# Twenty-four further loads of V behind the last DMA transpose, ahead of eleven output stores on one queue

## The chip, the cores and the metric

The kernel runs on one core of a Trainium2 chip. The core has a matrix engine (TensorE, PE in the profile), a vector engine (VectorE, DVE), a scalar engine (ScalarE, ACT), GpSimd (POOL) and SyncE (SP), which issues almost all DMAs here. The engines run side by side and each works through its own instructions in order; between engines only semaphores order the work. Sixteen DMA engines move data between HBM and SBUF. The metric is the device time of one execution in microseconds (us), lower is better.

## The reference

One block of a transformer with conditioned layer norms, 2048 positions of 512 features in bfloat16. What is computed:

```python
mod = (_silu(c) @ w_mod).reshape(c.shape[0], 6, 1, -1)      # sa, ca, ga, sb, cb, gb
h = _layernorm(x) * (1 + ca) + sa
x = x + ga * _A_ref(h, A_wqkv, A_wo)      # attention
h = _layernorm(x) * (1 + cb) + sb
x = x + gb * _B_ref(h, B_w1, B_w3, B_w2)  # silu(h @ w1) * (h @ w3) @ w2, inner width 1792
```

The attention has 32 heads of 16 features, and each position sees eight positions only, itself and those 2, 4, ... 14 before it:

```python
idx = pos[:, None] - off[None, :]         # off = arange(8) * 2
vg = v[:, :, idx_c, :].reshape(B, H, S, W, Dh)
o = jnp.einsum('bhsw,bhswd->bhsd', attn, vg)
```

## The kernel before, in words

The positions are cut into 16 tiles T of 128. Layer norm, projections to Q, K and V, attention, the second layer norm and the two-layer network are each written as functions over tiles or groups of tiles, which record operations (`Program.op`, `Program.dma`) with what they read and write. The order of all operations and the buffer that each value gets are then not decided when the kernel is built: they stand in two long lists, ORDER and SLOTS (L952 and L998). `place` follows them, `synchronize` derives the waits on semaphores from them, and `emit` (L208) writes, for every engine, its operations in that order, each with its waits ahead of it. So each engine, SP included, has one fixed sequence.

V goes through HBM: after its projection each tile is stored to `v_scratch_dram` (L695), and the attention loads it back with the eight needed rows beside each other (L790). One such load is 128 runs of 2 KB (256 KB), and four make a tile's buffer `sb_vsh` of 128 x 8 x 512; there are two of these buffers, `vshb`, and a third in the space of the finished weights (`sb_vshx`). In each load a row of V is read up to eight times, since neighbouring positions need the same rows.

At the end stand the network's two layers. L853 multiplies the activations with w1 or w3 (four 128x256 matmuls make one group and fill half a PSUM bank), L859 on ACT and L862 on DVE turn two groups into one `sb_hh`, and L891 or L879 multiply these with w2. L901 on DVE adds the residual and writes an output buffer `sb_o`, and SP stores it:

```python
p.op("dve", lambda e: e.tensor_tensor(vo.at[:, 0:n], bank(vz)[:, 0:n], x_sb[:, T, c0:c0 + n], ALU.add),
     c_dve(n), ("zo", T), r=[vz, vx[T]], w=[vo])
finals.append(p.dma(out2d[T * P:(T + 1) * P, c0:c0 + n], lambda: vo.at[:, 0:n], ("zo", T), (128, 2 * n), r=[vo], cost=400, store=True))
```

There are four output buffers, called here the first to the fourth, and eight PSUM banks. A value that gets a buffer or a bank waits for all users of the value that had it before (`o.prev` in `place`).

The end of the sequences matters for the change. SP has, as its last entries: four DMA transposes of `sb_xn` into `sb_h` (for the second layer norm of tiles 12 to 15, the last of them being the program's last transpose); then the stores of the tiles 9 (from the fourth output buffer), 11 (second), 10 (third), 12 (third), 13 (second), 1 (first) and 8 (fourth); then four stores of half tiles, two each of tiles 14 and 15. DVE has the L901 of tiles 10, 9 and 11, then of tile 8, which writes the fourth output buffer again, then those of tiles 13 and 12, then four for the halves; the L862 lie between them. The L901 of tile 8 reads PSUM bank 1. The next user of that bank on PE is an L853 group for tiles 14 and 15: the eighth group of four behind the w2 matmuls (L891) that the trace starts at 213.20.

Of the kernel before, what the change touches and what calls it, by code (L numbers as in the profile page):

```python
# [10 lines left out]
P = 128  # L11
S = 2048
D = 512
H = 32
DH = 16
W = 8
DIL = 2
# [4 lines left out]
PAD = 16  # L22
# [51 lines left out]
class Program:  # L74
# [133 lines left out]
    def emit(self):  # L208
        nc = self.nc
        with nc.Block() as block:  # L210
            starter = {"sp": block.sync, "pe": block.tensor, "dve": block.vector, "act": block.scalar,
                       "pool": block.gpsimd}
            for eng in ENGINES:
                todo = self.order[eng]
                if not todo:
                    continue

                def section(e, todo=todo, eng=eng):
                    for o in todo:
                        for d in o.waits:  # L220
                            e.wait_ge(d.inc[0], d.inc[2])
                        ins = o.fn(e)
                        if o.inc is not None:
                            ins.then_inc(o.inc[0], o.inc[1])
                    if eng == "sp":
                        for d in self.final:
                            e.wait_ge(d.inc[0], d.inc[2])

                starter[eng](section)

# [5 lines left out]
def bass_adaLN_cond__sliding_local_dilated__glu_gated_swiglu__prompt_kernel(  # L236
    nc, A_x, A_wqkv, A_wo, B_x, B_w1, B_w3, B_w2, c, w_mod, out
):
    ctx = ExitStack()
    with ctx:  # L240
        p = Program(nc, ctx)
        _build(p, *[_full_ap(t) for t in (A_x, A_wqkv, A_wo, B_w1, B_w3, B_w2, c, w_mod, out)])
        p.place(ORDER, SLOTS)
        p.synchronize()
        p.emit()
# [27 lines left out]
def _build(p, A_x, A_wqkv, A_wo, B_w1, B_w3, B_w2, c, w_mod, out):  # L273
    nc, ctx = p.nc, p.ctx
# [5 lines left out]
    def sb(shape, dtype, name):  # L280
        return ctx.enter_context(nc.sbuf_tensor("sb_" + name, shape, dtype))
# [12 lines left out]
    vshb = [sb([P, 8, D], bf, f"vsh{i}") for i in range(2)]  # L294
# [44 lines left out]
    v_dram = nc.dram_tensor("v_scratch_dram", (PAD + S, D), bf)  # L339
# [97 lines left out]
    for g in range(NG):  # L437
# [8 lines left out]
         r=[vthc, vcT], w=[vc4])  # L446
# [3 lines left out]
         r=[vc4, vident] + wm_hold, w=[vpc])  # L450
# [494 lines left out]
    for o, n in zip(p.late, GATES):  # L945
        if n >= 0:
            o.deps[p.gates[n]] = True
    p.final = finals


GATES = [-1, -1, -1, -1, -1, -1, -1, -1, -1, 1, -1, -1, -1, -1, -1, 1, -1, -1, 2, -1]
# [94 lines left out]
```

## Time and profile before

| what | us |
|---|---|
| median of 2 runs | 243.95 (242.89 to 245.02) |
| the profiled execution, device time | 243.86 |
| its span, first to last instruction | 242.0 |
| PE busy | 232.3 |
| DVE busy | 180.0 |
| ACT busy | 135.6 |
| last transpose issued | 199.04 |
| first output store behind it issued | 210.31 |

The span is what the profile's times count from; the device time has 1.86 us more around it. "Busy" counts an engine's compute instructions; waits and the issuing of DMAs are not counted, so SP, which only waits and issues, appears with its issues alone (as SPq). A line such as L853 is the line of the kernel that made the instruction. In a timeline row the first number is the start, the second the time that the row covers, and "x" the count of instructions merged in it; an idle time before the row and what ended it stand in brackets. In the sums by window the busy times of the engines follow each other, and the last three columns are the granted TensorE clock, the busy share of the DMA engines and the GB/s that they moved.

### The profile page before, as it was taken

What the parts mean: (1) busy time and instruction counts of PE and PEld (TensorE: products, weight loads), DVE (VectorE), ACT (ScalarE), POOL (GpSimd) and SP (SyncE); (2) the same over time, 40 slices, a digit from 0 to 9 for tenths busy, and PEclk for the clock granted to TensorE, in tenths of its full rate; (3) what the DMA queues carried; (4) which work ended last, traced back from release to release, by engine and by line L of the source; (5) the groups of instructions that cost most, each with busy time, mean ns of one, the idle gap of its engine ahead of it and who ended that gap; (6) DMA issues with size and microseconds to landing.
All of it is one profiled execution on the core that took longest, in us unless ns stands there. A gap on an engine that the chain in (4) does not pass through costs nothing.

```text
span 242.0 us, 4516 instructions
## 1 busy us (share of the span) xinstructions
PE 232.3 (96%) x1778; PEld 135.8 (56%) x1803; DVE 180.0 (74%) x278; ACT 135.6 (56%) x269; POOL 23.2 (10%) x66
## 2 busy tenths in 40 slices
PE   7999999979899999999999999999999999999995
PEld 2667454434368777674444454444444555768864
DVE  4689999968899999999999999928443611433532
ACT  2178498757979743794774479262476334314200
POOL 4144110002003000040000012000010100000000
PEclk9999999999999999999999999999999999999999
DMA  6998999899999879698292189674031010010004
GB/s 219 385 355 286 172 257 264 132 253 261 305 323 285 228 199 237 148 270 176 71 242 80 33 172 240 141 174 131 3 103 27 0 24 22 23 45 0 3 0 130
DMA packets 45756, 38.84 MB, mean 160 GB/s; under 512 B 21656, under 2 KB 36520, under 8 KB 45736
## 3 DMA queue, kind: packets, MB, share of 16 engines
q1 hardware_dynamic: 45728, 38.56, 61.6%
q8 instruction: 14, 0.23, 0.4%
q14 instruction: 6, 0.05, 0.1%
q10 hardware_dynamic: 8, 0.00, 0.0%
HBM read 29.62 MB, written 4.21 MB: 140 GB/s over the span
## 4 chain that ended last, share of the span: by engine, by line
PE 73%; DVE 13%; DMA 6%; SPq 3%; ACT 1%; issue 1%; POOL 0%; DVEq 0%; ACTq 0%
PE pall L853 39%; PE pall L891 17%; DVE sb_pq L712 5%; PE pall L837 4%; DMA sb_vsh<-v_scratch_dram 3%; SPq L124 3%; PE pall L825 2%; PE pall L497 2%; PE pall L879 2%; DVE sb_vsh L797 2%; DVE sb_st L534 2%; DMA sb_wo<-in_A_wo_dram 2%; DMA v_scratch_dram<-sb_v 2%; PE pall L722 2%; PE pall L661 1%
## 5 line engine op out<-in xcount | busy, mean ns | idle before, releaser
L853 PE MATMUL pall<-sb_h,sb_w 128*128 128x256 bf16 (+1 forms) x665 | 102.7, 307 | 0.9 <-ACT sb_sg L859 0.4
L853 PEld LDWEIGHTS pall<-sb_h,sb_w 128*128 128x128 bf16 x672 | 64.6, 98 | 36.0 <-issue 1.3
L859 ACT ACTIVATE sb_sg<-pall 128x256 bf16<-128x256 f32 (+1 forms) x84 | 35.1, 455 | 49.1 <-PE pall L853 44.4
L862 DVE TENSOR_TENSOR sb_hh<-sb_sg,pall 128x256 bf16<-128x256 bf16 (+1 forms) x84 | 39.6, 506 | 29.0 <-PE pall L853 27.1
L891 PE MATMUL pall<-sb_w,sb_hh 128*128 128x512 bf16 x187 | 43.3, 379 | 0.5
L712 DVE TENSOR_TENSOR sb_pq<-sb_q,sb_kT 128x4096 bf16<-128x4096 bf16 x16 | 36.4, 2285 | 0.0
L661 PE MATMUL pall<-sb_h,sb_wqkv 128*128 128x512 bf16 (+1 forms) x156 | 31.6, 335 | 1.6 <-ACT sb_h L591 0.7
L797 DVE TENSOR_TENSOR sb_vsh<-sb_vsh,sb_al 128x4096 bf16<-128x4096 bf16 x13 | 29.7, 2288 | 3.2 <-DMA sb_vsh<-v_scratch_dram 1.9
L891 PEld LDWEIGHTS pall<-sb_w,sb_hh 128*128 128x128 bf16 x196 | 19.0, 98 | 20.7 <-issue 0.4
L591 ACT ACTIVATE sb_h<-sb_h,sb_modc 128x512 bf16<-128x512 bf16 (+1 forms) x24 | 16.4, 737 | 15.7 <-DMA sb_h<-sb_xn 15.6
L661 PEld LDWEIGHTS pall<-sb_h,sb_wqkv 128*128 128x128 bf16 x160 | 14.7, 98 | 13.6 <-ACT sb_h L591 1.3
L901 DVE TENSOR_TENSOR sb_o<-pall,sb_x 128x512 bf16<-128x512 f32 (+1 forms) x18 | 11.1, 628 | 14.4 <-PE pall L891 11.7
L681 PE MATMUL pall<-sb_wqkv,sb_h 128*128 128x512 bf16 x63 | 16.5, 379 | 0.1
L837 PE MATMUL pall<-sb_wo,sb_ot 128*128 128x512 bf16 x61 | 15.6, 379 | 1.0 <-DMA sb_ot<-sb_ac 0.8
L556 POOL TENSOR_SCALAR sb_nm<-sb_sx 128x2 f32<-128x2 f32 x8 | 2.7, 332 | 129.0 <-DVE sb_x L841 129.0
L614 ACT ACTIVATE sb_h<-pall,sb_modc 128x256 bf16<-128x256 bf16 (+1 forms) x18 | 10.3, 629 | 7.8 <-PE pall L606 7.8
L831 ACT ACTIVATE sb_ac<-pall 128x512 bf16<-128x512 f32 x16 | 9.4, 601 | 7.6 <-PE pall L825 7.5
L571 ACT ACTIVATE sb_xn<-sb_x,sb_nb,sb_rs 128x512 bf16<-128x512 bf16 x16 | 12.6, 810 | 1.6 <-POOL sb_nb L569 1.4
L841 DVE SCALAR_TENSOR_TENSOR sb_x<-pall,sb_x 128x512 bf16<-128x512 f32 x16 | 10.7, 686 | 3.6 <-PE pall L837 3.6
L534 DVE BATCH_NORM_STATS2 sb_st<-sb_x 128x6 f32<-128x512 bf16 x16 | 10.7, 669 | 2.2 <-DMA sb_x<-in_A_x_dram 2.2
L671 ACT ACTIVATE sb_kT<-pall 128x512 bf16<-128x512 f32 (+1 forms) x18 | 9.6, 566 | 4.6 <-PE pall L661 4.6
L560 ACT ACTIVATE sb_xn<-sb_x,sb_nm 128x512 bf16<-128x512 bf16 x16 | 11.6, 725 | 0.7 <-POOL sb_nm L556 0.6
(86 smaller groups left out, 202.1 us busy)
## 6 DMA issues: line engine op xcount, KB each, us to landing
sb_vsh<-v_scratch_dram SPq DMA_DIRECT2D x52, 256.0 KB, 4.5
sb_w<-in_B_w_dram SPq DMA_DIRECT2D x6, 512.0 KB, 5.0
sb_vshx<-v_scratch_dram SPq DMA_DIRECT2D x12, 256.0 KB, 5.0
sb_w<-in_B_w_dram SPq DMA_DIRECT2D x6, 384.0 KB, 4.4
v_scratch_dram<-sb_v SPq DMA_DIRECT2D x16, 128.0 KB, 4.1
out_dram<-sb_o SPq DMA_DIRECT2D x14, 128.0 KB, 1.8
sb_wqkv<-in_A_wqkv_dram SPq DMA_DIRECT2D x4, 384.0 KB, 7.7
sb_x<-in_A_x_dram SPq DMA_DIRECT2D x3, 512.0 KB, 7.8
```

The source lines that it names most:

```text
L534: o = p.op("dve", lambda e, T=T: e.bn_stats(st[:, T, :], x_sb[:, T, :]), 595, ("st", T), r=[vx[T]], w=[vs])
L571: p.op("act", lambda e, vn=vn, T=T: e.activation(vn.at[:], x_sb[:, T, :], ACT.Identity, bias=nb[:, T, :], scale=rs[:, NT + T, :]), c_act(5 ...
L591: return e.activation(vh.at[:, ft, 0:n * P], vh.at[:, ft, 0:n * P], ACT.Identity, bias=modc[:, 8 * which + ft:8 * which + ft + 1], scale=m ...
L661: ins = e.matmul(bank(vp)[:, j * n:(j + 1) * n], wqkv[:, t, col:col + P], vh.at[:, t, 0:n], start=(t == ORDER[0]), stop=(t == ORDER[-1]))
L681: ins = e.matmul(bank(vp), vh.at[:, t, tt * P:(tt + 1) * P], wqkv[:, t, 2 * D:3 * D], start=(t == ORDER[0]), stop=(t == ORDER[-1]))
L712: return e.tensor_tensor(vp.at[:], in0, in1, ALU.mult)
L797: return e.tensor_tensor(v_w, v_w, a_w, ALU.mult)
L837: ins = e.matmul(bank(vy), vt.at[:, ft, :], wo[:, ft, :], start=(ft == 0), stop=(ft == KT - 1))
L853: ins = e.matmul(bank(vp)[:, 0:n], wt[:, t, fi * P:(fi + 1) * P], vh.at[:, t, 0:n], start=(t == 0), stop=(t == KT - 1))
L859: p.op("act", lambda e: e.activation(vt.at[:, 0:n], bank(vgp)[:, 0:n], ACT.Silu), c_act(n), k, r=[vgp], w=[vt], table="silu")
L862: p.op("dve", lambda e: e.tensor_tensor(vh_.at[:, 0:n], vt.at[:, 0:n], bank(vup)[:, 0:n], ALU.mult), c_dve(n), k, r=[vt, vup], w=[vh_])
L891: ins = e.matmul(bank(vz), vhh[fi].at[:, tt * P:(tt + 1) * P], w2[:, fi, :], start=(fi == 0), stop=(fi == NF - 1))
```

## The change

After SP's last DMA transpose, `emit` now waits for its landing and calls a new function `patterns`. It issues 24 loads from `v_scratch_dram` into the two buffers `vshb`, which nothing reads any more at that point, in five rounds; after each round SP waits until all loads so far have landed. Behind the last wait SP goes on with its output stores as before. At the end SP also waits for the semaphore of the loads. The orders of PE, DVE, ACT and POOL and all else on SP are as they were.

The rounds: (1) six loads of 256 KB in the form of the kernel's own V loads, of tile 9; (2) three loads of 512 KB, each partition p taking four rows of 1 KB that begin at its own row and lie two rows apart; (3) one load of 1 MB, each partition p taking eight rows in one run of 8 KB, beginning at row 2p; (4) six loads of 256 KB of 2 KB runs in which no row repeats; (5) eight loads of 128 KB of single rows of 1 KB.

```diff
                 def section(e, todo=todo, eng=eng):
+                    last_turn = max((o.pos for o in todo if o.dma and o.key[0] == "tr"), default=-1)
                     for o in todo:
...
                         if o.inc is not None:
                             ins.then_inc(o.inc[0], o.inc[1])
+                        if eng == "sp" and o.pos == last_turn:
+                            e.wait_ge(o.inc[0], o.inc[2])
+                            self.patterns(e)
                     if eng == "sp":
                         for d in self.final:
                             e.wait_ge(d.inc[0], d.inc[2])
+                        e.wait_ge(self.extra, self.extra_level)
...
     p.final = finals
+    p.extra = p.ctx.enter_context(nc.semaphore("extra"))
+    p.extra_level = 0
+
+    def patterns(e):
+
+        done = [0]
+
+        def load(to, src):
+            e.dma_start(to, src).then_inc(p.extra, 16)
+            done[0] += 16
+
+        def settle():
+            e.wait_ge(p.extra, done[0])
+
+        def rows(T, r=0):
+            return (PAD + T * P + r) * D
+
+        for i in range(6):
+            q = i % 4
+            load(vshb[i // 4][:, 2 * q:2 * q + 2, :], bass.AP(v_dram, rows(9, 32 * q), [[2 * D, 16], [-DIL * D, W], [1, 2 * D]]))
+        settle()
+        for i in range(3):
+            load(vshb[i % 2][:, 4 * (i // 2):4 * (i // 2) + 4, :], bass.AP(v_dram, rows(9, 8 * (i // 2) - 14), [[D, P], [2 * D, 4], [1, D]]))
+        settle()
+        load(vshb[0][:], bass.AP(v_dram, rows(8), [[2 * D, P], [1, 8 * D]]))
+        settle()
+        for i in range(6):
+            q = i % 4
+            load(vshb[i // 4][:, 2 * q:2 * q + 2, :], bass.AP(v_dram, rows(6 + 2 * q), [[2 * D, 16], [32 * D, W], [1, 2 * D]]))
+        settle()
+        for i in range(8):
+            load(vshb[0][:, i, :], bass.AP(v_dram, rows(4 + i), [[D, 16], [16 * D, 8], [1, D]]))
+        settle()
+        p.extra_level = done[0]
+
+    p.patterns = patterns
```

## The prediction

> **What bounds the kernel now.** I read the page's busy shares first, then the chain that ended last, and from there only the last 45 us, since the diff touches nothing ahead of the last transpose.
>
> ```profile
> PE 232.3 (96%) x1778; PEld 135.8 (56%) x1803; DVE 180.0 (74%) x278; ACT 135.6 (56%) x269; POOL 23.2 (10%) x66
> PE 73%; DVE 13%; DMA 6%; SPq 3%; ACT 1%; issue 1%; POOL 0%; DVEq 0%; ACTq 0%
> ```
>
> PE is busy 96% of the span and is 73% of the chain that ended last. The DMA side is nearly idle at the end (the page's DMA row ends in small digits), so the bytes of the new loads compete with little. What matters is where they stand: on SP, in order, ahead of eleven output stores. The timeline of SP shows that place, with the count of stores before the long pause of SP and after it:
>
> ```profile
> 197.81 2.50 SPq L124 DMA_TRANSPOSE sb_h<-sb_xn  x2
> 210.31 1.40 SPq L124 DMA_DIRECT2D out_dram<-sb_o  x3
> ```
> ```profile
> 236.01 4.20 SPq L124 DMA_DIRECT2D out_dram<-sb_o  x8
> ```
>
> The second of those transposes is issued at 199.04, and the view of that window gives 2.4 us to its landing: 201.44. From there SP has nothing to do until 210.31, issues three stores, and is idle again until 236.01. Next, who needs those three stores. The timeline of DVE has the L901 that write the output buffers:
>
> ```profile
> 203.62 0.69 DVE L901 TENSOR_TENSOR sb_o<-pall,sb_x 128x512 bf16<-128x512 f32 x1 [8.05 <-PE pall L891]
> ...
> 209.60 1.28 DVE L901 TENSOR_TENSOR sb_o<-pall,sb_x 128x512 bf16<-128x512 f32 x2
> ...
> 217.31 0.69 DVE L901 TENSOR_TENSOR sb_o<-pall,sb_x 128x512 bf16<-128x512 f32 x1
> ```
>
> By the order and the slots, the first three are tiles 10, 9 and 11, and their stores are SP's three. The one at 217.31 is tile 8. It writes the same output buffer as tile 9, so it waits for tile 9's store, the first of the three. That store is issued at 210.31 and lands 1.7 us later (the DMA view of that window), at 212.0: today 5.3 us of slack. And PE:
>
> ```profile
> 213.20 2.97 PE L891 MATMUL pall<-sb_w,sb_hh 128*128 128x512 bf16 x13
> 216.01 13.26 PE L853 MATMUL pall<-sb_h,sb_w 128*128 128x256 bf16 x120
> ```
>
> From 216.01 PE runs groups of four L853 without a gap, 0.109 us each (13.26 over 120, with a little overlap), 0.437 a group. By the slots the eighth group writes the PSUM bank that tile 8's L901 reads, so it waits for that L901. It starts at 216.01 + 7 x 0.437 = 219.07; the L901 ends at 218.00. So PE can do 1.07 us more before a late L901 stops it, and PE issues in order: it stops altogether.
>
> **The change, part by part.** Nothing is removed. SP gets, behind the transpose that lands at 201.44, a wait for it and five rounds of loads, each closed by a wait for its landing; three stores and then eight stand behind them.
>
> *Bytes.* Round 1: 6 x 262,144 = 1.57 MB; round 2: 3 x 524,288 = 1.57; round 3: 1.05; round 4: 1.57; round 5: 8 x 131,072 = 1.05. Together 6.8 MB.
>
> *What one round costs.* Two rates and one lone load carry it, from the sums by window and from the DMA view of 84.8 to 85.4:
>
> ```profile
> 6.70:12.90 6.20, 5.80 (x69) 4.28 (x70) 4.44 (x15) 1.03 (x2) 1.08 (x3) 1.00 1.06 379
> 75.00:84.00 9.00, 8.95 (x82) 7.50 (x80) 8.98 (x13) 7.80 (x20) 1.09 (x3) 1.00 1.00 265
> ```
> ```profile
> sb_vsh<-v_scratch_dram SPq DMA_DIRECT2D x1, 256.0 KB, 3.0
> ```
>
> The last columns are the DMA share and GB/s. Between 6.7 and 12.9 plain loads of inputs flow, each byte read once: 379. Between 75 and 84 only loads of V flow that read every row again up to eight times, in the pattern of round 1: 265, so 0.99 us for one. The lone load of that kind, issued on an idle queue at 84.92, lands after 2.95 us (the trace's landing; the view rounds it): 0.99 of transport and 1.96 fixed. Rounds 1, 2 and 3 read rows repeatedly (eight, four and four times), so I give them 265; round 4 reads every row once, so 379; round 5 too, but there the issues bind: an issue on a free queue takes 0.48 (the gap between the whole-tile stores after 236), on a loaded one 0.6 to 0.64, and the last of eight lands about 2.5 after its issue (1.96 and 131,072 bytes at 265).
>
> Round 1: 1.96 + 5.94 = 7.9 (six such loads issued from 100.06 on landed within 8.5, with a transpose before them). Round 2: 7.9. Round 3: 1.96 + 3.96 = 5.9. Round 4: 1.96 + 4.15 = 6.1, about what six issues of 0.6 and a landing give. Round 5: 7 x 0.53 + 2.5 = 6.2. The sum is 34.0 us, so SP is held from 201.44 to **235.4**.
>
> *Bounds.* Fast: all rounds at 379 and issues of 0.48: 6.1 + 6.1 + 4.7 + 6.1 + 5.7 = 28.7, end at 230.1. Slow: the repeated reads at 225 GB/s, the lowest rate of a stretch of V loads (87.9 to 93, transposes among them), round 4 at 265 and issues of 0.64: 34.0 + 2.8 + 1.8 + 0.8 = 39.4, end at 240.8. How 1 KB rows read four times, or 8 KB runs, flow is in no row; I take the V loads as the nearest.
>
> *What of it is hidden.* The block is free up to 215.6, which is 217.31 less the 1.7 of the store: 14.2 us, while SP would idle. Past that, everything counts. Tile 9's store goes at 235.4, lands at 237.1, tile 8's L901 takes 0.69 and ends at 237.8, and PE's eighth group starts then and not at 219.07: **+18.7 us**. What is queued behind the held L901 are 17 L862 and six L901, all in order on DVE; behind PE's eighth group stand the other L853 and the last L891 and L879. After the release DVE needs 0.33 a group against PE's 0.44, so PE sets the pace as before and nothing of the delay is won back. The eight last stores keep their distance to PE.
>
> *A cost behind it: the clock.* PE stands still for 18.7 us, which it does nowhere in the trace. What a cold PE costs shows at the start, in the chain in order of time:
>
> ```profile
> 1.51 5.30 PE pall L497 x12
> ```
>
> Twelve 128x512 matmuls take 5.3 us, 0.43 each, while the L891 above take 0.216 to 0.23 each (13 in 2.97). So PE ran at half pace for its first 5.2 us and lost 2.6. After an idle stretch the loss lies between 0 (the clock stays) and 2.6; I take 2.6, since that row is also PE out of idleness. The Trainium skill ("TensorE: Matmul & The Clock Gate", Part 1: The HAM clock gate) says that about 3.4 us of idleness halve the clock and about 3.4 us of activity restore it, an estimated loss of 1.7 to 2.6 by the phase of its window; with 1.7 the time would be 264. No row inside the span shows such a fall.
>
> *Sum.* 18.7 + 2.6 = 21.3 us. The profiled execution took 243.86 us (span 242.0 and 1.86 around it), so 265.2; the median of the runs, 243.95, is 0.1 above it. Forecast: **265**, 8.7% slower.
>
> **Rivals.**
> *Loads at plain pace.* If reading a row again costs nothing when nothing else runs on the queues, all rounds go at 379 and the hold ends at 230.1: +13.4 and 2.6, so 260; without the loss of clock 257.3. For it: the stretch at 265 ran beside busy PE, DVE and ACT. Against: its DMA share is 1.00 and only loads of V flowed. The skill's rule ("SBUF — State Buffer", The DMA setup-cost knee) of about 2 us and 436 GB/s per transfer would end the hold still earlier, an estimated 257 in time; the 265 of this trace speaks against it. Chance 0.14.
> *Repeated reads of new shape at half pace.* If rounds 2 and 3 draw many engines onto the same rows worse than round 1 does, at 132 GB/s they cost 13.9 and 9.9, 10 more: 275. For it: 265 against 379 shows that repeats cost something already. Against: round 2 spreads over more rows than a V load. Chance 0.13.
> *Not slower: the hold ends before anybody needs the store.* Decided at 215.6. It would take 6.8 MB and five fixed parts in 14.2 us, over 484 GB/s with no fixed part at all; the highest slice of the page's GB/s row is 385. It would give 243.9. Chance 0.02.
> Something unseen, 0.03. My own forecast (260.5 to 271) keeps 0.68.
>
> **How the numbers follow.** The range goes from the fast bound without loss of clock, 257, to the slow bound with it, 265.2 + 5.4 = 270.6, and a little over: 257 to 272. It holds the forecast and the first rival, 0.82; 0.18 are out. About 2% is what a measurement of this kernel can tell from no change: faster 0.01, same 0.02, slower 0.97.
>
> **What would show it.** In the new profile: the 24 loads at L962 begin at about 201.5, in five bursts of 7.9, 7.9, 5.9, 6.1 and 6.2; the first store behind them is issued near 235.4; the L901 of tile 8 is released by a DMA of sb_o after some 19 us of idle DVE; PE has one gap from 219.1 to 237.8 ahead of an L853; the PEclk row dips once behind it; the 22 us from PE's restart to its end keep their length but for 2.6. It would be wrong if PE's gap began elsewhere (another buffer or bank decides), if the bursts had other lengths, or if the loads slowed work ahead of 217.

## The result, and the profile after

The changed kernel took 266.55 us (median of 2 runs, 265.58 to 267.53) against 243.95; the ratio is 1.093, 95% interval 1.066 to 1.119. Run again beside other kernels (4 runs of it, 13 of the kernel before) it took 266.43 against 243.78: 1.091, interval 1.083 to 1.099. The times here and below are medians of all executions, but the ratios and intervals compare only those in the faster of the two states that executions fall into, so a ratio can be up to 0.9% off the quotient of the two times beside it. The profiled execution took 267.53, with a span of 265.7.

The diff adds five lines ahead of the functions, so L853 is now L858, L862 is L867, L891 is L896 and L901 is L906; L962 is the new loads (the kernels of some experiments shift these by one or two again). The page of the changed kernel, shares and chain:

```profile
PE 233.7 (88%) x1778; PEld 136.2 (51%) x1803; DVE 180.1 (68%) x278; ACT 135.4 (51%) x269; POOL 24.0 (9%) x66
...
PEclk9999999999999999999999999999999998556999
...
PE 57%; DMA 19%; DVE 12%; SPq 7%; ACT 2%; issue 2%; POOL 0%; DVEq 0%; ACTq 0%
```

PE has 1.4 us more of busy time and 23.7 us more of span: it waits. In the chain that ended last, DMA went from 6% to 19% and SP from 3% to 7%. The PEclk row has a dip that it did not have. The dip did not stop PE: PE is idle from 220.97 on, and the granted clock over 222.9 to 231.0, where PE does nothing, is 0.53.

The timelines of the changed kernel, SP, then DVE, then PE (start, time covered, what; idle time before and its releaser in brackets):

```profile
199.55 2.50 SPq L124 DMA_TRANSPOSE sb_h<-sb_xn  x2
203.18 32.88 SPq L962 DMA_DIRECT2D sb_vsh<-v_scratch_dram  x24
238.16 1.33 SPq L124 DMA_DIRECT2D out_dram<-sb_o  x3
```
```profile
218.39 0.75 DVE L867 TENSOR_TENSOR sb_hh<-sb_sg,pall 128x256 bf16<-128x256 bf16 x2 [2.60 <-PE pall L858]
239.94 0.69 DVE L906 TENSOR_TENSOR sb_o<-pall,sb_x 128x512 bf16<-128x512 f32 x1 [20.80 <-DMA out_dram<-sb_o]
```
```profile
217.75 3.22 PE L858 MATMUL pall<-sb_h,sb_w 128*128 128x256 bf16 x28
240.69 11.79 PE L858 MATMUL pall<-sb_h,sb_w 128*128 128x256 bf16 x92 [19.71 <-DVE sb_o L906]
```

This is the whole mechanism in three steps. SP issues the first of the three stores at 238.16, where before it was 210.31. DVE's L906 of tile 8 is released by the landing of a store. PE does 28 matmuls, which is seven groups of four, and then waits for that L906; the run of 120 L853 of the kernel before is cut into 28 and 92.

The execution also was 1.7 us late before the change could act: its last transpose is issued at 200.78, before it was 199.04. That is scatter: in the repeat of the same kernel (span 263.4) the loads begin at 201.37, and over all kernels below their start lies between 200.9 and 203.2 in no relation to what was changed (for e5, which loads later, the transpose's landing is meant).

### The profile page after: what moved, and what is told of

Same layout as the page of the kernel before. It is cut to its first block, busy times and chain, and to the rows that moved or that the text cites. A ratio compares the mean times of both kernels' runs of the same rounds, so it can differ in the third digit from the quotient of the medians.

```text
span 265.7 us, 4541 instructions
## 1 busy us (share of the span) xinstructions
PE 233.7 (88%) x1778; PEld 136.2 (51%) x1803; DVE 180.1 (68%) x278; ACT 135.4 (51%) x269; POOL 24.0 (9%) x66
## 4 chain that ended last, share of the span: by engine, by line
PE 57%; DMA 19%; DVE 12%; SPq 7%; ACT 2%; issue 2%; POOL 0%; DVEq 0%; ACTq 0%
PE pall L858 32%; DMA sb_vsh<-v_scratch_dram 12%; PE pall L896 11%; DVE sb_pq L717 4%; SPq L962 4%; PE pall L842 4%; SPq L124 3%; DMA sb_wm_s<-in_w_mod_dram 2%; PE pall L830 2%; PE pall L884 2%; DMA sb_wo<-in_A_wo_dram 2%; DVE sb_st L539 2%; DVE sb_vsh L802 2%; PE pall L727 1%; DMA v_scratch_dram<-sb_v 1%
## 5 line engine op out<-in xcount | busy, mean ns | idle before, releaser
L858 PE MATMUL pall<-sb_h,sb_w 128*128 128x256 bf16 (+1 forms) x665 | 104.6, 311 | 20.6 <-DVE sb_o L906 19.7
L858 PEld LDWEIGHTS pall<-sb_h,sb_w 128*128 128x128 bf16 x672 | 65.2, 99 | 57.0 <-DVE sb_o L906 20.1
L867 DVE TENSOR_TENSOR sb_hh<-sb_sg,pall 128x256 bf16<-128x256 bf16 (+1 forms) x84 | 39.6, 505 | 29.5 <-PE pall L858 27.8
L896 PE MATMUL pall<-sb_w,sb_hh 128*128 128x512 bf16 x187 | 43.3, 379 | 0.5
L906 DVE TENSOR_TENSOR sb_o<-pall,sb_x 128x512 bf16<-128x512 f32 (+1 forms) x18 | 11.1, 628 | 35.5 <-DMA out_dram<-sb_o 21.7
L896 PEld LDWEIGHTS pall<-sb_w,sb_hh 128*128 128x128 bf16 x196 | 19.0, 98 | 20.7 <-issue 0.4
```

The costliest lines, as they stand in the source:

```text
L858: ins = e.matmul(bank(vp)[:, 0:n], wt[:, t, fi * P:(fi + 1) * P], vh.at[:, t, 0:n], start=(t == 0), stop=(t == KT - 1))
L867: p.op("dve", lambda e: e.tensor_tensor(vh_.at[:, 0:n], vt.at[:, 0:n], bank(vup)[:, 0:n], ALU.mult), c_dve(n), k, r=[vt, vup], w=[vh_])
L896: ins = e.matmul(bank(vz), vhh[fi].at[:, tt * P:(tt + 1) * P], w2[:, fi, :], start=(fi == 0), stop=(fi == NF - 1))
```

## Experiments

**Whose place is it? The three stores from another queue (e1).** All loads stay.

```diff
-finals.append(p.dma(..., r=[vo], cost=400, store=True))
+finals.append(p.dma(..., r=[vo], cost=400, store=True, eng="act" if T in (9, 10, 11) else "sp"))
```

> All 24 loads stay as in the change; only the three stores of tiles 9, 11 and 10 are issued from ACT, so they no longer stand behind the loads on SP. My theory (SP's order holds tile 9's store, tile 8's L901 waits for it, PE for that L901): the hold still runs from 201.4 for 35.0 us to 236.4, but the next store behind it is due at 236.0, so only 0.4 us of it shows; ACT waits for the L901 at 209.6 to 210.9 and issues three DMAs of some 0.4 us each, which may set PE back by up to 1.5. Time 244 to 246, no PE gap near 219. Rival (the 6.8 MB of loads, or the long wait as such, slow the work beside them): 262 to 268 still.

Measured: 246.87 against 244.92, ratio 1.015 (1.000 to 1.029). PE's run is whole again, and what DVE waits for is another store, at the end:

```profile
215.44 13.26 PE L858 MATMUL pall<-sb_h,sb_w 128*128 128x256 bf16 x120
```
```profile
DVE sb_o L906 <- DMA out_dram<-sb_o: 4.0, 1, 4.0
```

So the 6.8 MB beside PE cost nothing that PE shows; some 20 of the 22.6 us went with the place of three stores. The two or so that remain are more than I had written (the forecast ended at 246); the interval reaches down to no change. The stores now mix with the loads: by the DMA view of 209.7 to 211.5 they land after 5.6 us (median) instead of 1.7, and round 2 lasts 8.9 instead of 6.9, so the hold, which begins at 200.9, ends at 237.6 and not 35.0 later, at 235.9.

```profile
out_dram<-sb_o ACTq DMA_DIRECT2D x3, 128.0 KB, 5.6
```

**Is it the output buffer? A fifth one for tile 8 (e2).**

```diff
     for v, s in zip(self.pooled(), slots, strict=True):
         v.slot = s
+    [v for v in self.pooled() if v.name == "o"][8].slot = 104
...
     opool = Pool("o", [])
+    opool.items[104] = sb([P, D], bf, "o4")
```

> All as in the change, but tile 8's L901 writes a fifth output buffer of its own, so it waits for no store. My theory: PE runs through at 219; the hold to 236.4 then meets the L901 of tiles 13 and 12 (due at 234.7), which wait for the stores of tiles 11 and 10 (issued at 236.9 and 237.3, landing at 238.7 and 239.2), and the half tiles wait for the stores behind those; worked through store by store the last lands at 245.4 instead of 241.4: +4, time 248 (246 to 250), without a lowered clock. Rival (another buffer, or a bank, or SP's hold itself stops PE): 264 to 268.

Measured: 249.14 against 244.92, ratio 1.025 (1.011 to 1.038): +4.2. SP is held as in the change (201.06 to 236.79, 35.7 us against 35.0), and PE's run of 120 is whole. L908 is here what L906 is in the change. DVE's waits in that kernel:

```profile
DVE sb_o L908 <- DMA out_dram<-sb_o: 6.5, 2, 4.6
```

The long wait of 20.8 has become 4.6 and 1.9 at the end. One buffer of 1 KB per partition thus takes out some 18 us; the hold of SP does not stop PE by itself, but only through the buffer that tile 8 shares with tile 9.

**Does the hold cost in proportion, or from a point on? Rounds left out (e3, e4).**

The calls of `load` and `settle` for the other rounds are taken out of `patterns`: e3 has rounds 1 and 3 only, e4 rounds 1, 2 and 3 only.

> Only rounds 1 and 3 of the loads (7 loads, 2.6 of the 6.8 MB). In the changed kernel's profile they take 8.4 and 4.5 us, so SP is held to 214.3, which is before 215.6, from where on the delay counts. My theory: nothing shows, 243 to 245. Rival (every us of hold, or every MB, costs in proportion: 22.6 us for 35.0): 12.9/35.0 of it, +8.3, 252.

Measured: 244.40 against 244.92, ratio 1.002 (0.998 to 1.006). Seven loads and a hold of SP of 12.9 us cost nothing. The timeline of SP in e3:

```profile
201.34 8.76 SPq L962 DMA_DIRECT2D sb_vsh<-v_scratch_dram  x7
214.27 21.98 SPq L124 DMA_DIRECT2D out_dram<-sb_o  x4
```

The first store goes at 214.27 and its buffer is needed at 217.2: 1.7 of landing leave 1.2 us unused.

> Rounds 1, 2 and 3 only (10 loads, 4.2 MB), 8.4 + 6.9 + 4.5 = 19.8 us, so SP is held to 221.2. My theory: tile 9's store lands at 222.9, tile 8's L901 ends at 223.6, PE's gap runs from 219.1 to 223.7: +4.6, and 0 to 1.6 for a lowered clock behind a gap of 4.6: 248.5 to 250.2. Rival (proportional to the hold): +12.8, 257.

Measured: 251.49 against 244.92, ratio 1.036 (1.018 to 1.054): +6.6, a little over the 6.2 of the upper end, and 1.3 over the 250.2 that was written. PE's row and the sums by window behind it (the third number from the right is the granted clock):

```profile
224.63 11.88 PE L858 MATMUL pall<-sb_h,sb_w 128*128 128x256 bf16 x92 [4.44 <-DVE sb_o L906]
```
```profile
220.30:224.50 4.20, 0.00 (x0) 0.00 (x0) 0.61 (x2) 0.59 (x2) 0.00 (x0) 1.00 0.49 178
224.60:228.50 3.90, 3.87 (x21) 2.85 (x22) 1.39 (x4) 0.77 (x2) 0.00 (x0) 0.57 0.00 0
228.60:246.00 17.40, 17.35 (x147) 14.26 (x146) 6.87 (x17) 3.13 (x9) 0.00 (x0) 1.00 0.09 31
```

PE's run starts at 216.98 here, so its eighth group was due at 220.04 and starts 4.6 late, as worked out. The 92 L858 behind take 11.9 instead of 10.2 (13.26 less 28 x 0.109): 1.7 for the clock. The granted clock is still 1.00 during the gap and falls when PE works again. A gap of 4.4 us is enough for a price of 1.7.

**The same loads elsewhere on SP (e5, e8).** In e5 they stand behind the three stores; in e8 rounds 1 and 3 stay ahead of the stores and rounds 2, 4 and 5 go behind them.

```diff
# e5, against the change
-                    last_turn = max((o.pos for o in todo if o.dma and o.key[0] == "tr"), default=-1)
+                    last_turn = max((o.pos for o in todo if o.dma and o.key == ("zo", 10)), default=-1)
...
                         if eng == "sp" and o.pos == last_turn:
-                            e.wait_ge(o.inc[0], o.inc[2])
                             self.patterns(e)
```

> The same 24 loads, moved on SP from ahead of the three stores of tiles 9, 11 and 10 to just behind them (from 211.7 on). My theory: tile 8's L901 and PE are not held, PE ends at 239.3 as before; the hold of 35.0 us now ends at 246.7 and meets the last eight stores, due at 236.0: they and the half tiles' L901 behind them come 10.7 later, time 254.6 (253 to 257), and PE has a gap only near its end if at all. Rival (the loads cost the same wherever they stand among the stores): 266.

Measured: 256.11 against 243.78, ratio 1.047 (1.039 to 1.054): +12.3. SP is held from 213.25 to 247.99, and this wait of DVE shows the new place:

```profile
DVE sb_o L905 <- DMA out_dram<-sb_o: 12.3, 1, 12.3
```

PE never stops. This execution was 1.5 us late before the loads began (its run of 120 L857 starts at 217.51, not 216.01), so the store behind the hold was due at 237.5 and came 10.5 late. With the late start that is 12.0 of the 12.3 by which this execution is longer than the profiled one of before; the medians differ by as much, but how late the other executions started is not on record.

> All 24 loads on SP, but put where SP has time: rounds 1 and 3 (8.4 + 4.5 us) behind the last transpose, rounds 2, 4 and 5 (6.9 + 8.1 + 7.1) behind the three stores of tiles 9, 11 and 10. My theory (only what reaches past a due store counts): the first hold ends at 214.3, before 215.6, and costs nothing; the second runs from 215.7 for 22.1 to 237.8, 1.8 past the next store's due time of 236.0: +1.8, time 245.7 (244.5 to 247.5), no PE gap, no lowered clock ahead of the end. Rival (the loads' cost goes with their bytes or count): 266.

Measured: 246.54 against 245.00, ratio 1.008 (1.005 to 1.012). All 24 loads on the same queue, and 1.5 us (by the medians) to 2.0 (by the ratio) instead of 22.6:

```profile
213.87 1.31 SPq L124 DMA_DIRECT2D out_dram<-sb_o  x3
215.22 19.98 SPq L964 DMA_DIRECT2D sb_vsh<-v_scratch_dram  x17
237.29 4.09 SPq L124 DMA_DIRECT2D out_dram<-sb_o  x8
```

SP's two idle stretches of the kernel before, 201.4 to 210.3 and 211.7 to 236.0, take them almost whole; the excess over the second one, 237.29 against 236.0, or 1.5 when PE's run is taken as the mark (it starts 0.24 earlier here), is what the time shows.

**The same loads from another engine (e6).**

```diff
-if eng == "sp" and o.pos == last_turn:
-    e.wait_ge(o.inc[0], o.inc[2])
-    self.patterns(e)
+if eng == "pool":
+    last = [o for o in self.order["sp"] if o.key[0] == "tr"][-1]
+    e.wait_ge(last.inc[0], last.inc[2])
+    self.patterns(e)
```

> The same 24 loads and waits, issued from POOL, which has nothing else to do then, behind the same wait for the last transpose; SP only waits for their end at its own end. My theory: SP's stores go as before, PE has no gap; the end moves only if POOL's loads last beyond 241.4, that is over 40 us instead of 35.0; unknown pace there, so 243.5 to 250. Rival (the traffic itself slows the stores or the engines): the stores' landing of 1.7 us and PE's 0.109 us per L853 grow, 255 or more.

Measured: 246.86 against 243.78, ratio 1.011 (1.007 to 1.015): +2.7 to +3.1. PE's run of 120 takes 13.26 again. The stores that fall among the loads do get slower: of those issued between 236 and 238 the median lands after 3.6 instead of 1.8.

```profile
out_dram<-sb_o SPq DMA_DIRECT2D x4, 128.0 KB, 3.6
```

The chain that ended last runs over one of these stores, which lands after 3.83; the last load is issued by 237.7 and its round lands after 2.5, so it is not the loads' own end that shows. So traffic has a price, on the stores, of some 2 to 3 us at the end; not on PE. Half of the rival's condition came true (the landing grew), its time did not.

**What a round costs (e7, e9).** The sum of the rounds had come out well, its terms less so. Two kernels measured loads alone, one execution each (298.66 and 287.85); their time is not used.

> A measurement of the disputed cost: in place of the five rounds, six rounds of six 256 KB loads that differ in the source alone, then single loads on an idle queue. In order: (a) round 1's pattern, rows read eight times; (b) round 4's, no row twice, 2 KB runs 32 KB apart across neighbouring partitions; (c) the same 2 KB runs in linear order; (d) one 2 KB run read by eight partitions; (e) 1 KB runs, linear; (f) 2 KB runs of w_mod 6 KB apart; then three loads of 512 KB and two of 1 MB, linear. Theory 1 (reading a row again is what makes V loads slow, as I had put it): (a) and (d) take 8 us or more, (b), (c), (f) about 6.1. Theory 2 (the spread of the 2 KB runs, as in b, costs as much as repeats): (a) and (b) 8 or more, (c) and (f) 6 to 6.5, (d) unclear. Theory 3 (a DMA of 256 KB has its own fixed cost in the stream of some 0.3 us whatever its source): all six rounds at 7.5 to 8.5, and the large loads at 400 GB/s behind a fixed part. The time is of no use here: the loads hold SP for over 50 us.

> A second measurement of the loads alone, linear sources unless said: three single 256 KB loads each waited for, three single ones of round 4's pattern, three of round 1's; then six of 256 KB, three of 512 KB (the same bytes), two of 1 MB, and six of round 4's pattern. From the run before (six linear ones 7.2 us, a single 512 KB 3.5, a single 1 MB 4.7): if a load's size sets the pace (a fixed cost per load in the stream), singles take 2.6, 3.3 and 3.1; six linear 7.2, three of 512 KB 5.9, two of 1 MB 7.1. If bytes alone do (a stream of linear loads runs at about 290 GB/s however it is cut), three of 512 KB take 7.2 too and two of 1 MB 9.2. The time is of no use: the loads hold SP for some 50 us.

From the first issue to the last landing, us:

| six loads of 256 KB, source | e7 | e9 |
|---|---|---|
| (a) round 1's: rows read eight times | 7.9 | |
| (b) round 4's: no row twice in a load | 8.5 | 8.2 |
| (d) one run for eight partitions | 8.1 | |
| (c) linear 2 KB runs | 7.2 | 6.8 |
| (e) linear 1 KB runs | 7.3 | |
| (f) w_mod, 2 KB runs 6 KB apart | 7.0 | |
| three linear loads of 512 KB (the same bytes) | | 6.5 |
| two linear loads of 1 MB | | 7.3 |

None of the three theories holds as written. Theory 1 falls: (b) repeats nothing within a load and is no faster than (a), and (d), which reads one run eight times, lies between. (Over the kernels here the same six loads scatter by half a microsecond: (a) takes 7.8 to 8.4 and (b) 8.1 to 8.5.) What (a), (b) and (d) share, and (c), (e) and (f) don't, is the form of the source, 16 x 8 x run instead of one row per partition. The single loads in e9 show it best; this is its chain in order of time, a linear one, then (b), then (a):

```profile
202.40 2.69 DMA sb_vsh<-v_scratch_dram
...
210.29 3.25 DMA sb_vsh<-v_scratch_dram
...
220.25 3.21 DMA sb_vsh<-v_scratch_dram
```

The three of each kind average 2.62, 3.30 and 3.19: the 16 x 8 form costs some 0.6 more for a load by itself, whatever rows it names, and some 1 for six in a row. The trace of e9 also has the packets, 128 of 2 KB for each of these loads. From the first packet's start to the last one's end they take 1.2 to 1.4 us in both forms (1.8 in one load of (b), the slowest), but the first starts 0.96 us after the issue with the linear source and 1.3 with the other, and the landing follows the last packet by 0.3 against 0.4 to 0.6. So the 0.6 lies ahead of the packets and behind them, not in moving the bytes. The issue shows the form as well: on an idle queue it takes SP 0.33 for a linear load and 0.51 for the others. Size matters in a stream: by the landings, the loads behind the first come every 0.85 us at 256 KB (308 GB/s), every 1.5 at 512 KB (350) and 2.4 at 1 MB (433, from one pair). Of the two readings written down for e9, bytes alone falls: two loads of 1 MB take 7.3, where it gave 9.2 and the fixed cost per load 7.1. Three loads of 512 KB take 6.5, between the 5.9 of the one and the 7.2 of the other, so the fixed cost per load isn't right in size either.

**The change once more (e0).**

> The changed kernel once more, for an interval beside the others: 265 to 267.5, PE's gap of 19.7 us again behind 28 L853 of its run, the granted clock at half for some 3 us behind it.

Measured: 266.43, as told above; span 263.4, PE's idle time 19.41 behind 28 L858.

## Why the prediction was right, point by point

The forecast was 265 with a range of 257 to 272 and slower by 8.7%; measured are 266.4 to 266.6, 9.1% to 9.3%.

*Who waits for whom* was right in every link. The changed kernel shows each (SP's first store, the L906 released by a store, the cut behind seven groups), and two experiments took links away: another queue for the stores (e1) and another buffer (e2) each bring PE's run of 120 back.

*The free part* was put at 14.2 us up to tile 8's L901 and 1.07 more until PE needs it, 15.3 together. In e3 12.9 us of hold change nothing. In the kernels with longer holds, the hold less the delay of PE's eighth group is 15.1 each time: 19.7 less 4.6 in e4, 35.0 less 19.9 in the change, 34.7 less 19.6 in its repeat, and 56.3 less 41.2 in e9. So beyond the free part the delay of PE does grow one to one.

*The length of the hold* was put at 34.0 and measures 35.0 (34.7 in the repeat). Its terms erred both ways. The chain in order of time of the changed kernel has the last load of each round, and the two steps behind them:

```profile
206.32 5.25 DMA sb_vsh<-v_scratch_dram
...
212.57 5.87 DMA sb_vsh<-v_scratch_dram
218.46 4.46 DMA sb_vsh<-v_scratch_dram
...
226.07 4.96 DMA sb_vsh<-v_scratch_dram
...
235.46 2.69 DMA sb_vsh<-v_scratch_dram
238.16 1.75 DMA out_dram<-sb_o
```

| round | put at | measured |
|---|---|---|
| 1 | 7.9 | 8.4 |
| 2 | 7.9 | 6.9 |
| 3 | 5.9 | 4.5 |
| 4 | 6.1 | 8.1 |
| 5 | 6.2 | 7.1 |

The step that failed is the one that gave rounds 1 to 3 a rate of 265 GB/s because they read rows again, and round 4 379 because it does not. Round 4 behaves as round 1, which has its form; rounds 2 and 3 have larger loads and a simpler source and are faster than put. The two rows behind the rates, 265 and 379, differ in more than in repeats: the first is of 16 x 8 loads of 256 KB, the second mostly of input loads of 384 KB and more, and a stream of linear 256 KB loads runs at 308. Round 5 is bound by the issues, as said, but each took 0.64 from one to the next and not 0.53. The five errors, +0.5, -1.0, -1.4, +2.0 and +0.9, cancel to +1.0; that the sum came out is luck in part.

*The rivals.* That of *half pace* (275) put rounds 2 and 3 at 13.9 and 9.9; they took 6.9 and 4.5, so it is out. That of *plain pace* (260) is out by its hold of 28.7, which measured 35.0; but its premise, that reading a row again costs nothing, is what e7 and e9 bear out. What it had wrong is the pace of 379 for loads of the 16 x 8 form. The rule of the Trainium skill ("SBUF — State Buffer", The DMA setup-cost knee), about 2 us and 436 GB/s, gives as an estimate 2.6 for a load of 256 KB, 3.2 for 512 KB and 4.4 for 1 MB. The single linear loads measure 2.6, 3.5 to 3.6 and 4.7, near it; for six loads of 256 KB the estimate is 5.6, and the runs show 6.8 to 7.2 for linear ones and 7.8 to 8.5 for the 16 x 8 form.

*What is behind the release*: +18.7 was forecast. PE's eighth group was due at 217.75 + 28 x 0.109 = 220.81 and started at 240.69: +19.9, the 1.0 of the hold and 0.2 of steps between store, L906 and PE. DVE won nothing back, as argued. (The 0.33 that DVE was said to need for a group is for two, since two groups make one `sb_hh`, so DVE had more room than written.)

*The clock* was mis-sized: 2.6 was taken, 1.6 is measured (92 L858 take 11.79 instead of 10.2). The sums by window of the changed kernel:

```profile
240.70:244.00 3.30, 3.30 (x16) 2.37 (x17) 1.33 (x4) 0.77 (x2) 0.00 (x0) 0.51 0.00 0
244.00:262.00 18.00, 17.95 (x153) 14.79 (x153) 6.92 (x17) 3.13 (x9) 0.00 (x0) 1.00 0.09 30
```

PE worked at 0.51 for 3.3 us and at full clock behind that. The row that I took the price from, 5.2 us of half pace at the start of the kernel, was a longer spell than this one; and in that row the half pace shows in the durations alone, for the granted clock reads 1.00 there. The clock also fell during the gap and not only behind it, as the 0.53 between 222.9 and 231.0 shows.

But a price of 2.6 does occur. The same 92 L858 behind a gap take 11.58 in the repeat (a price of 1.4, gap 19.4), 11.65 in e9 (1.5, gap 41.0), 11.88 in e4 (1.7, gap 4.4), and in e7:

```profile
270.99 12.78 PE L858 MATMUL pall<-sb_h,sb_w 128*128 128x256 bf16 x92 [50.99 <-DVE sb_o L906]
```

That is a price of 2.6, with the granted clock at 0.50 from 271.0 to 276.2. So the price lies between 1.4 and 2.6 and does not follow the length of the gap; which of these a run gets, no row of the kernel before shows. The estimate that it worked out from the Trainium skill's "TensorE: Matmul & The Clock Gate" (Part 1: The HAM clock gate), 1.7 to 2.6, holds for e4 and e7; the change, its repeat and e9 lie 0.1 to 0.3 below it.

Sum: 19.9 + 1.6 = 21.5, against 21.3 forecast. The hold came out 1.0 longer than put and the clock 1.0 cheaper, so that the sum is this close is luck once more. The profiled execution is 23.7 longer than that of before. Of this, 1.7 is the late start told above, and the other 0.5 lies behind the landing of the last store, at the end of SP's program; its cause stays open. The repeat, which has no late start, took 265.2 in its profiled execution.

Two slips of the prediction touch neither its sum nor a chance: 6.8 MB in 14.2 us is 480 GB/s and not 484, and round 4 reads no row twice within a load, but its last two loads read the rows of its first two again.

## What to carry to other kernels

A DMA that nobody needs still held every DMA behind it on its queue, because the issuing engine waited for its landing: ask not what the transfer costs but which later entry of that queue is due first, and who waits for it. The free time is the idle stretch of the queue up to that due time, less the landing and plus the slack of whoever waits; here, up to there the added work cost nothing, beyond it every us showed up one to one, and then the stopped matrix engine added its lowered clock. The same 24 loads cost 22.6 us, 12.3, or some 2 depending only on where they stood on the queue, and one more output buffer (4.2 us left) or another issuing engine (some 3 left) hid most of it.

## What the runs showed of the hardware that was not expected

- Reading rows of HBM eight times over is not what makes the V loads slow. The form of the source costs some 0.6 us for a load by itself (3.2 to 3.3 against 2.6 for 256 KB), ahead of the first packet and behind the last; whether that is time to make the addresses or something else, the runs don't tell.
- Behind a gap of 4.4 us in PE's work the granted clock fell only when PE was busy again, for 3.4 us; behind gaps of 19.4, 19.7, 41.0 and 51.0 us it was low already and stayed so for 2.8, 3.3, 3.0 and 5.3 us more. In these five executions the price does not grow with the wait.
- Stores that ran among loads landed 2 to 4 us later (3.6 in e6 and 5.6 in e1 against 1.7 to 1.8), while the matrix engine's pace of 0.109 us a matmul did not change beside 6.8 MB of loads.
